# Token weights loaded behind the last quad's keys and queries, zero matmuls only on long-free banks, and a re-planned order in a fused attention and mixer kernel

## The chip, the cores and the metric

One core of one Trainium2 chip. The metric is the device time of one execution in microseconds (us), the median of several. A profiled execution also gives a span, which is about 1.7 us shorter than the metric.

## The reference

Sigmoid attention for 8 batches, 12 heads, 448 positions of 64 features, followed by a token-mixing and a channel-mixing MLP with residuals:

```
scores = q @ k.T / sqrt(64) - log(448);  x = sigmoid(scores) @ v        # x: (8, 448, 768)
h  = relu(x.T @ w_tok1) @ w_tok2                                        # over positions, 256 wide
u  = x + h.T
out = u + relu(u @ w_ch1) @ w_ch2                                       # over channels, 1536 wide
```

## The kernel before

The kernel does not write its instructions in the order of its source. It records operations, each with its engine, an estimated duration, what it waits for and the buffers it uses. A planner then plays them through on estimated times, and the instructions are emitted in the order of the planned starts. Each engine then runs its own list in that order. "Quad" below is four heads: three per batch. The matmuls of scores ("S") and values ("V") use 64x64 tiles of the array, nearly all else the whole array.

The parts that matter:

```python
# Plan: landings of loads, with hitches at some points of the load pipe; landings of what SyncE (SP) issues
self.far, self.load_far, self.sp_wait = 5.0, 2.0, 2.0
self.hitch = [(8.6, 1.1), (15.2, 1.0), (21.9, 0.8)]
...
elif e == "SP":                              # stores, and the transposes done by DMA
    free[e] = t + o.us
    o.end = t + self.far + min(5.0, max(0.0, self.pipe - t - 0.5))
...
self.log.sort(key=lambda o: o.start)         # the order in which everything is emitted
for o in self.log:
    o.emit()

# the kernel: the order of the first loads
load_early(0, "q", "k")
load_early(1, "k", "q")
load_early(0, "v")
tok1_ld = load_w_tok1()
tok2_ld = load_w_tok2()                      # VectorE then spreads it: "spread0/1/6"
load_early(2, "k", "q")
load_early(1, "v")
load_early(2, "v")

# choose(): when nothing else is ready in the first 21 us, a zero matmul (a "fill") keeps TensorE busy
if 3.0 < t < FILL and (not cands or min(c[0] for c in cands) > t + 0.12) and up.start is not None:
    if any(x <= t for x, _ in plan.free_slots("bank", up)):
        o = fill["op"] = filler()            # writes a PSUM bank, reads zeros

# token(b): u becomes fp16 on ScalarE and is transposed by a DMA that SyncE issues; channel1(b) needs all of uT
uT_ops[b].append(op(f"uT_{b}_{blk}", "SP", 1.3, turn, [o], [u16, uT[b]], rank=-1))
```

LEAD and SPAN set how far the scores of batches 2 to 7 run ahead of the mixer work, REST and PAUSE how token-mixing matmuls are spaced. All four only permute work.

## Time and profile before

| | |
|---|---|
| median before the change | 375.59 us (375.43 to 375.96, 3 runs) |
| profiled span | 374.0 us |
| TensorE busy | 366.1 us |
| matmuls, zero matmuls among them | 3,199, of these 20 fills and 7 at the very start |
| TensorE's listed waits | 3.6 us, of these 0.5 us after 45 us |

The prediction shows the lines.

### The profile page before, as it was taken

How to read it: one execution, taken by the hardware profiler on the slowest of the kernel's cores; microseconds unless marked ns; L12 is line 12 of the kernel's file. 1: busy time of each engine (PE TensorE's matmuls, PEld its weight loads, DVE VectorE, ACT ScalarE, POOL GpSimd, SP SyncE). 2: the span in 40 equal slices, each digit the busy share in tenths (PEclk: the TensorE clock that was granted, in tenths of full speed). 3: DMA queues.
4: the chain of work that ended last, by engine and by line, in shares of the span. 5: the costliest groups of instructions: out<-in, count | busy, mean ns of one | idle time of the engine just before them, and what ended most of it. 6: DMA issues, size and time to landing. Idle time of an engine off the chain costs nothing.

```text
span 374.0 us, 7992 instructions
## 1 busy us (share of the span) xinstructions
PE 366.1 (98%) x3199; PEld 187.3 (50%) x3199; DVE 175.7 (47%) x414; ACT 207.6 (56%) x269; POOL 116.0 (31%) x261
## 2 busy tenths in 40 slices
PE   8999999999999999999999999999999999999995
PEld 4455345554454554454445555444455555555653
DVE  4366345654433635552354243934462257665221
ACT  5896993386777877876765576575665321100000
POOL 8873236344444434534444342332000000000000
PEclk9999999999999999999999999999999999999999
DMA  6999999799998999999999999977014363400344
GB/s 102 170 181 206 209 209 183 111 175 178 123 153 147 175 180 137 153 147 227 122 142 131 216 157 193 174 115 107 6 25 104 91 149 88 72 0 2 84 102 110
DMA packets 97013, 50.06 MB, mean 134 GB/s; under 512 B 70544, under 2 KB 93456, under 8 KB 96976
## 3 DMA queue, kind: packets, MB, share of 16 engines
q0 software_dynamic: 24080, 21.62, 42.4%
q1 hardware_dynamic: 72656, 27.62, 41.1%
q8 instruction: 25, 0.41, 0.5%
q10 hardware_dynamic: 240, 0.31, 0.2%
q14 instruction: 12, 0.10, 0.1%
HBM read 43.45 MB, written 11.01 MB: 146 GB/s over the span
## 4 chain that ended last, share of the span: by engine, by line
PE 91%; DMA 3%; POOL 2%; DVE 1%; ACT 1%; issue 1%; SPq 0%; DVEq 0%; POOLq 0%
PE c L1007 30%; PE c L1066 29%; PE qk L578 10%; PE xa L616 8%; PE yn L933 5%; PE k L857 3%; DMA w_tok_s<-in_moe_w_tok_dram 2%; DMA out_dram<-ut 1%; PE xb L675 1%; POOL k L329 1%; PE k L707 1%; PE k L817 1%; PE tk L524 1%; PE k L841 1%; PE yt L891 1%
## 5 line engine op out<-in xcount | busy, mean ns | idle before, releaser
L594 ACT ACTIVATE attn<-qk,att_bias 128x896 f16<-128x896 f32 (+1 forms) x172 | 161.9, 988 | 75.5 <-PE qk L578 75.1
L1007 PE MATMUL c<-uT,w_ch 128*128 128x448 f16 x576 | 119.2, 353 | 0.5 <-DMA out_dram<-ut 0.5
L1066 PE MATMUL c<-w_ch,h2aT 128*128 128x384 f16 x576 | 99.6, 326 | 0.1
L1023 DVE TENSOR_SCALAR h2aT<-c 128x384 f16<-128x384 f32 x96 | 53.5, 557 | 72.9 <-PE c L1007 72.7
L1007 PEld LDWEIGHTS <-w_ch 128*128 128x128 f16 x576 | 52.8, 98 | 57.0 <-issue 12.4
L1066 PEld LDWEIGHTS <-h2aT 128*128 128x128 f16 x576 | 55.0, 98 | 40.8 <-issue 5.9
L1079 DVE TENSOR_TENSOR u<-u,c 128x384 f32<-128x384 f32 x48 | 26.6, 554 | 71.1 <-PE c L1066 65.8
L578 PE MATMUL qk<-qT,kT 64*64 64x448 f16 x672 | 53.5, 363 | 0.6 <-ACT qT L547 0.3
L616 PE MATMUL xa<-attn,v 64*64 64x448 f16 x672 | 36.7, 350 | 0.0
L781 POOL COPY mark<-attn 1x1 f16<-1x1 f16 x54 | 9.6, 178 | 82.8 <-ACT attn L594 80.8
L578 PEld LDWEIGHTS <-kT 64*64 64x64 f16 x672 | 14.9, 104 | 32.7 <-issue 30.1
L496 POOL COPY qp<-q 128x384 f16<-128x384 f16 (+1 forms) x54 | 21.3, 431 | 20.6 <-DMA q<-in_q_dram 13.3
L955 DVE TENSOR_TENSOR u<-x,yn 128x384 f32<-128x384 f16 x48 | 24.7, 548 | 4.8 <-PE yn L933 4.7
L963 ACT ACTIVATE u<-u 128x768 f16<-128x768 f32 x21 | 17.7, 842 | 15.4 <-DVE u L955 15.4
L653 ACT ACTIVATE xT<-xa 128x448 f16<-128x448 f32 (+2 forms) x61 | 22.2, 441 | 6.7 <-PE xa L616 5.4
L616 PEld LDWEIGHTS <-v 64*64 64x64 f16 x672 | 19.5, 107 | 11.9 <-DMA q<-in_q_dram 0.4
L496 POOL COPY kp<-k 128x384 f16<-128x384 f16 (+1 forms) x54 | 21.2, 428 | 10.8 <-DMA k<-in_k_dram 10.8
L933 PE MATMUL yn<-h,w_tok 128*128 128x384 f16 x104 | 21.6, 327 | 0.1
L1023 DVE TENSOR_SCALAR h2odd<-c 128x64 f16<-128x64 f32 x96 | 20.6, 215 | 0.0
L1066 PE MATMUL c<-w_ch,h2odd 128*128 128x384 f16 x96 | 17.1, 326 | 0.1
L340 POOL DMA_DIRECT2D q<-in_q_dram x21 | 15.1, 718 | 6.4 <-issue 6.1
L340 POOL DMA_DIRECT2D k<-in_k_dram x21 | 15.1, 719 | 6.0 <-issue 3.9
(73 smaller groups left out, 207.1 us busy)
## 6 DMA issues: line engine op xcount, KB each, us to landing
out_dram<-u SPq DMA_DIRECT2D x48, 192.0 KB, 3.1
k<-in_k_dram POOLq DMA_DIRECT2D x21, 224.0 KB, 5.1
q<-in_q_dram POOLq DMA_DIRECT2D x21, 224.0 KB, 5.4
v<-in_v_dram POOLq DMA_DIRECT2D x21, 224.0 KB, 5.3
w_ch<-in_moe_w_ch_dram POOLq DMA_DIRECT2D x6, 768.0 KB, 19.2
out_dram<-ut SPq DMA_DIRECT2D x6, 192.0 KB, 4.3
v<-in_v_dram POOLq DMA_DIRECT2D x6, 112.0 KB, 5.6
x<-xT SPq DMA_TRANSPOSE x32, 4.2
```

Of the source, the lines that this page charges most:

```text
L340: nc.gpsimd.dma_start(out=t.ap().rearrange("r h j e -> r h (j e)"), in_=heads.rearrange("(h s) (p j) e -> (s p) h (j e)", s=2, j=J),)
L496: nc.gpsimd.tensor_copy(out=pm[:, to, :, :], in_=src[:, fr, :, :])
L578: nc.tensor.matmul(out=ps[64 * s : 64 * s + 64, h, 0:S], lhsT=kT[64 * h : 64 * h + 64, i, s, :], rhs=qT[64 * h : 64 * h + 64, :, s, :], st ...
L594: nc.scalar.activation(out=at[:, hs, :], in_=ps[:, hs, 0:S], func=SIGMOID, bias=bias_t[:, :], scale=att_scale,)
L616: nc.tensor.matmul(out=ps[s](slice(64 * h, 64 * h + 64)), lhsT=vf[64 * s : 64 * s + 64, h, order[i], :], rhs=attn[i][64 * s : 64 * s + 64, ...
L653: nc.scalar.activation(out=xt[:, s, to : to + n], in_=ps[s](every)[:, fr : fr + n], func=COPYF)
L933: nc.tensor.matmul(out=ps[:, :], lhsT=w_tok2[:, t, s0 : s0 + 2, :], rhs=h1[b][:, t, c], start=(t == 0), stop=(t == 1),)
L955: nc.vector.tensor_tensor(out=to, in0=x, in1=y, op=ADD)
L1007: nc.tensor.matmul(out=ps[:, :], lhsT=w_ch1[cb // 4][:, db, 128 * (cb % 4) : 128 * (cb % 4) + 128], rhs=uT[b][:, db, :], start=(db == 0), ...
L1023: nc.vector.tensor_scalar(out=to, in0=ps[:, fr], scalar1=0.0, scalar2=None, op0=MAX)
L1066: nc.tensor.matmul(out=ps[:, :], lhsT=h, rhs=w, start=(cb == 0), stop=(cb == NCB - 1))
L1079: nc.vector.tensor_tensor(out=t, in0=t, in1=ps[:, :], op=ADD)
```

## The change

It is meant to let the planner fill the early gaps of TensorE with the transposes of the last quad instead of zeros, to keep zero matmuls from standing in front of real work while they wait for a bank, and to plan with landings nearer to the real ones.

```diff
-        self.hitch = [(8.6, 1.1), (15.2, 1.0), (21.9, 0.8)]
+        self.hitch = [(8.6, 1.1), (15.2, 1.4), (19.5, 0.8), (21.9, 0.5)]
...
-    LEAD, SPAN, REST, LATE = 18.0, 0.93, 1.0, 0
-    FILL, UP = 21.0, 7
+    LEAD, SPAN, REST, LATE = 20.0, 0.86, 0.8, 0
+    FILL, UP, SURE = 21.0, 7, 0.8
...
-    PAUSE = 1.0
+    PAUSE = 1.5
...
     load_early(0, "v")
+    load_early(2, "k", "q")
     tok1_ld = load_w_tok1()
     tok2_ld = load_w_tok2()
-    load_early(2, "k", "q")
     load_early(1, "v")
...
-            if any(x <= t for x, _ in plan.free_slots("bank", up)):
+            if any(x <= t - SURE for x, _ in plan.free_slots("bank", up)):
```

## The prediction

> **What bounds the kernel now.** I read the page's first lines, then the chain of waits, then the waits of TensorE, and last the timeline of the first 25 us of all engines. The time is 375.59 us, the profiled span 374.0.
>
> ```profile
> PE 366.1 (98%) x3199; PEld 187.3 (50%) x3199; DVE 175.7 (47%) x414; ACT 207.6 (56%) x269; POOL 116.0 (31%) x261
> PE 91%; DMA 3%; POOL 2%; DVE 1%; ACT 1%; issue 1%; SPq 0%; DVEq 0%; POOLq 0%
> ...
> 342.65 27.31 PE c L1066 x168
> ```
>
> The reader is to see that TensorE (PE) bounds nearly everything: it is busy in 366.1 of 374.0 us and makes 91% of the chain. The last line says how dense it is there: 27.31 us over 168 matmuls of 384 columns is 162.6 ns each. So no wait hides inside the stretches of plain matmuls; only the number of PE instructions, the switches between kinds of work, and PE's few waits can move. Those waits are listed in one view, for the whole run:
>
> ```profile
> PE idle L463 <- DVE att_bias L276: 1.2, 1, 1.2
> PE fill L478 <- DVE xT L647: 0.8, 1, 0.8
> PE c L1007 <- DMA out_dram<-ut: 0.5, 1, 0.5
> PE tk L524 <- issue: 0.3, 1, 0.3
> PE qk L578 <- ACT qT L547: 0.3, 1, 0.3
> PE qk L578 <- ACT uT L761: 0.3, 1, 0.3
> PE k L707 <- DVE h L724: 0.2, 1, 0.2
> ```
>
> They sum to 3.6 us, 1.2 of it the start that the change does not touch. The largest other one, 0.8 us, is what the change aims at. The timeline shows its cause (start, length, engine, line):
>
> ```profile
> 15.57 0.39 PE L478 MATMUL fill<-uT 128*128 128x256 f16 x2
> ...
> 16.21 0.72 PE L478 MATMUL fill<-uT 128*128 128x256 f16 x4
> 16.31 0.83 DVE L382 COPY w_tok<-w_tok_s 128x384 f16<-128x384 f16 x2 [3.21 <-DMA w_tok_s<-in_moe_w_tok_dram]
> ...
> 17.05 1.15 DVE L647 CAST xT<-xa 128x448 f16<-128x448 f32 x2
> ...
> 17.72 0.27 PE L478 MATMUL fill<-uT 128*128 128x256 f16 x1 [0.80 <-DVE xT L647]
> ```
>
> VectorE (DVE) sat 3.21 us for the second token weight to land at 16.3, with the two xT copies behind it in its order, although their matmuls were done by about 15.6. The zero matmul ("fill") wanted a PSUM bank that those copies free, so it stood in front of the next score matmuls until 17.72. ScalarE then lost 1.02 us too: its next sigmoid began at 18.36, after 17.34. Up to 17.34 its sigmoids run without a gap from 6.85, so there ScalarE is the bound and PE's fills cost nothing.
>
> **What the Trainium skill says.** (1) "TensorE: Matmul & The Clock Gate", the part on the array's detail and the step-by-step part: ScalarE and VectorE take their queue strictly in order, and matmuls keep program order, only weight loads being pulled ahead. The trace agrees: the copies waited behind a weight 3.21 us late, the scores behind a fill 0.80 us late. (2) The same page gives N columns / 2.4 GHz + about 2.5 ns for each warm matmul: 162.5 ns for 384 columns; the trace has 162.6. (3) The same page says that an idle window of about 3.4 us can halve the clock, which is why fills exist; this trace grants full clock in every slice and PE's longest wait is 1.2 us, so fewer fills should not cool it. (4) "TensorEngine Tiling (Array Packing)", key properties: changing the tiling mode drains the array. In the trace, from one group of three 448-column matmuls to the next with four 64x64 score matmuls between (chain at 38.53, 39.20, 39.51) takes 0.98 us; 3 x 0.189 + 0.19 (the score group where no switch borders it, at 21.32) is 0.76, so two switches cost 0.22, some 0.11 each.
>
> **The change part by part.** Comparing the built orders (no time in them):
>
> - Removed: fills fall from 20 to 9. All other kinds of PE work have the same counts (3,199 matmuls to 3,188). Four fills between scores at 14.23 to 14.88 took 0.65 us, less one switch of 0.11, so about 0.135 each. 11 x 0.135 = 1.5 us of PE work (1.2 by columns alone). Nine of the eleven stood after 13 us.
> - Switches between 64x64 and full-array work: 217 before, 215 after: 2 x 0.11 = 0.2 us. More groups of scores run straight into their value matmuls (22 against 18), which other splits nearly use up again.
> - Moved: keys and queries of the last quad of batch 0 go ahead of the token weights. Their transposes, 28 matmuls (at 18.79, 19.45 and 20.27: 0.34 + 0.51 + 0.29 = 1.14 us), now stand around the first scores of quad 1, where PE had fills. This is how the fills become useful; it is the same gain as theirs, not another.
> - Waits: VectorE's token-weight spread now stands after the xT copies and the x copy, so the 0.8 us should go. In its place the token weights come later: four loads of 112 KB are put ahead, 448 KB, at the 170 to 180 GB/s of those slices 2.6 us. The second weight then lands at about 16.3 + 2.6 = 18.9 (estimate). By hand along the new order: value matmuls done 15.6, xT copies until 16.9, x transposed 17.5, qT copy to 17.5, x copy to 18.35 (0.76 us); the first token matmul, now only one fill and one score group later, is there at about 17.7 and waits some 0.7. The spread ends at about 19.7, ReLU (0.42), second spread (0.6), second ReLU until 21.2; the first token-2 matmul arrives near 20.7 and waits some 0.5. So 0.8 goes, and 0.5 to 1.2 comes.
> - The planner's other numbers (LEAD, SPAN, REST, PAUSE) only permute PE work from 65 us on. Attention gets somewhat earlier: the scores of batch 6, quad 2 by 9 us of PE work, of batch 7 by 2 to 7. In the old run that quad's last transposed load was issued at 227.23, about 5 us to landing, used near 248: 16 us of slack, 9 of them spent. Some 0 to 0.3 us of new waits.
>
> Sum: -1.5 (fills) -0.2 (switches) -0.8 (the wait) +0.9 (new waits near 18 and 21 us) +0.2 (later) = -1.4 us. 375.59 - 1.4 = 374.2. After 45 us PE waits 0.5 us in all, so what is won at the start should keep to the end; the tail from the last matmul to the last store is unchanged.
>
> **The rivals.**
>
> - *The token weights' lateness eats it all.* For: the load is on the chain now (DMA 6.24 us at 10.05), and it is pushed back 2.6 us. Against: in the old order the first token matmul ran only at 21.8, and there was slack. If the wait is 2 us instead of 1.2, the time is about 375.
> - *Gain larger than the fills.* If the landing is as quick as planned and no new wait stands at 18 us, PE gains 1.5 + 0.2 + 0.8 = 2.5 us, giving 373.1. For: ScalarE also stops losing 1.02 us at 18.36, and bounds PE there.
> - *ScalarE or DMA becomes the bound in the squeezed middle.* ScalarE is busy 66.55 of 100 us between 150 and 250; DMA is at or above 9 tenths in most slices up to 260 us, which speaks for it. But loads are let go by sigmoids three units back, and the slack above is several us. Would add 0.5 to 2 us: 375 to 376.
> - *A colder clock after fewer fills*: would add a us or more at the start; no gap nears the window.
>
> **Range and chances.** The mechanisms move the time between -2.5 and about +0.3 us, so the range is 373.1 to 375.7. A change of 2% would be 7.5 us, while all of PE's waits and fills together are under 7 us: faster by 2% is nearly excluded, and slower by 2% would need a wait of a sort that nothing in the profile hints at.
>
> **What would show it.** Right: 9 fills, PE busy about 364.5 to 365, no fill waiting for xT, ScalarE's gap at 18.36 gone, the first group of 448-column channel matmuls (38.46 before) 1 to 2 us earlier, and a similar lead at 303 us and at the end. The token matmul should wait for the x copy for 0.3 to 1 us, and its second weight matmul for the spread or the ReLU. Wrong: a wait over 1.5 us on a token weight's landing or spread, waits on transposed keys or queries after 150 us, a granted clock under full, or a lead at 45 us that is lost later.

## More of the kernel before

A difference under half a us is near the scatter: the kernel before was between 374.8 and 376.2 us in nearly all of its executions, once 377.7.

One more place turned out to matter, a wait of TensorE (PE) at 174 us. In the kernel before, the timeline of SyncE and of PE there shows (start, length, engine, operation; in brackets the idle time before and its releaser):

```profile
167.25 1.26 SPq L501 DMA_TRANSPOSE qT<-qp  x1
168.60 1.22 SPq L991 DMA_TRANSPOSE uT<-u  x1
169.92 1.19 SPq L1044 DMA_DIRECT2D out_dram<-ut  x2
...
173.99 1.29 PE L1007 MATMUL c<-uT,w_ch 128*128 128x448 f16 x6 [0.52 <-DMA out_dram<-ut]
```

The channel matmuls of batch 3 wait 0.52 us, by the profile for an output store. They do not read what that store moves; what they do read is uT, whose last transpose was issued at 168.60.

## The result, and the profile after

375.23 us (375.05 to 375.62, 6 runs) against 375.69 us (375.35 to 376.03, 6 runs) of the kernel before: ratio 0.9989, 95% interval 0.9976 to 1.0002. Ratios here are the mean time of one kernel's runs over the mean of the runs of the kernel before that are listed beside it, so they are not quite the ratio of the medians. The time lies in the predicted range, 1.0 us above the predicted 374.2.

The page of the changed kernel, its line of engines and its chain:

```profile
PE 365.1 (98%) x3188; PEld 186.6 (50%) x3188; DVE 175.8 (47%) x414; ACT 207.8 (56%) x269; POOL 115.4 (31%) x261
PE 94%; DMA 2%; DVE 2%; ACT 1%; issue 0%; ACTq 0%
```

TensorE has 11 matmuls fewer and is busy 1.0 us less (busy time itself scatters: it is 367.1 us in experiment 8 and 366.0 in experiment 10, whose matmuls are those of the kernel before). The span is 0.6 us shorter. So part of the gain turned into waiting; PE's list of waits in the changed kernel says where:

```profile
PE c L1007 <- DMA uT<-u: 1.2, 1, 1.2
PE idle L463 <- DVE att_bias L276: 1.2, 1, 1.2
PE k L707 <- DVE h L724: 0.4, 1, 0.4
...
PE qk L578 <- ACT attn L594: 0.3, 1, 0.3
...
PE k L707 <- DVE x L691: 0.2, 1, 0.2
```

The fill's wait is gone. The two waits of token matmuls, for x (0.2) and for the ReLU (0.4), are those foreseen near 18 and 21 us. New and not foreseen is the first line. The start itself went as intended; the changed kernel's timeline of VectorE and PE:

```profile
16.20 1.16 DVE L647 CAST xT<-xa 128x448 f16<-128x448 f32 x2 [0.62 <-PE xa L616]
16.38 0.90 PE L578 MATMUL qk<-qT,kT 64*64 64x448 f16 x8
17.21 0.62 PE L675 MATMUL xb<-ident,xT 128*128 128x128 f16 x8
17.87 0.76 DVE L691 COPY x<-xb 128x512 f16<-128x512 f16 x2
18.57 1.04 DVE L382 COPY w_tok<-w_tok_s 128x384 f16<-128x384 f16 x2
```

The xT copies start right after their matmuls, ahead of the token weight's spread, which now starts at 18.57 (before: 16.31). Two score groups stand together at 16.38, the second of which had to wait until 17.92 before. The start of the first channel matmul, before and then after:

```profile
38.46 0.74 PE L1007 MATMUL c<-uT,w_ch 128*128 128x448 f16 x3
```

```profile
37.23 0.74 PE L1007 MATMUL c<-uT,w_ch 128*128 128x448 f16 x3
```

The changed kernel is 1.23 us earlier there, and has one group of two token matmuls more behind it (2 x 0.163 = 0.33 us), so its lead is 1.56 us in these two traces. At the end it is 0.6. Here is what took the rest, SyncE and then PE of the changed kernel:

```profile
172.46 1.18 SPq L1050 DMA_DIRECT2D out_dram<-u  x2
173.73 1.54 SPq L991 DMA_TRANSPOSE uT<-u  x1
175.38 1.25 SPq L501 DMA_TRANSPOSE kT<-kp  x1
176.72 1.24 SPq L991 DMA_TRANSPOSE uT<-u  x1
...
182.62 2.44 PE L1007 MATMUL c<-uT,w_ch 128*128 128x448 f16 x12 [1.21 <-DMA uT<-u]
```

It is the place of the 0.52 us wait before: the first channel matmuls of batch 3. ScalarE had finished the fp16 copy for that last transpose at 174.31 (173.47 + 0.84). SyncE was busy issuing others, each 1.2 to 1.5 us, and issued it at 176.72; it took 5.86 us to land. So the lead should have been lost in SyncE's order; the experiments test this. One of the signs that the prediction had named for being wrong, "a lead at 45 us that is lost later", has come.

### The profile page after: what moved, and what is told of

It is laid out like the page before. It is cut to its first block, busy times and chain, and to the rows that moved or that the text cites. A ratio compares the mean times of both kernels' runs of the same rounds, so it can differ in the third digit from the quotient of the medians.

```text
span 373.4 us, 7967 instructions
## 1 busy us (share of the span) xinstructions
PE 365.1 (98%) x3188; PEld 186.6 (50%) x3188; DVE 175.8 (47%) x414; ACT 207.8 (56%) x269; POOL 115.4 (31%) x261
## 4 chain that ended last, share of the span: by engine, by line
PE 94%; DMA 2%; DVE 2%; ACT 1%; issue 0%; ACTq 0%
PE c L1007 30%; PE c L1066 29%; PE qk L578 11%; PE xa L616 8%; PE yn L933 5%; PE k L857 3%; DMA uT<-u 2%; PE tq L524 1%; PE tk L524 1%; PE xb L675 1%; PE idle L463 1%; ACT attn L594 1%; PE k L817 1%; PE k L841 1%; PE k L707 1%; PE yt L891 1%
```

## The experiments

**Theory A**: the start gained 1 to 1.6 us, and a wait for the last uT transpose of batch 3, caused by SyncE's order, gave most of it back. **Rivals**: B, the DMA engines are saturated there and the landing does not follow the issue; L, the later numbers (LEAD and so on) are what matters; F, the predicted step that zero matmuls are work on the path, so that the gain is their number; K, zero matmuls hold TensorE's clock.

Edits that change only the order are made on the planned list, so everything else keeps its place. Eleven runs, the first eight runs on one chip, the last three on another. All were correct. The first call has 11 runs of the kernel before and the third has 11 of its own; experiments 5 to 8, of the second call, are compared with the 11 of the first call and one more.

**1. One swap on SyncE.**

```diff
-        self.log.sort(key=lambda o: o.start)
+        by = {o.name: o for o in self.log}; by["turnk_5_2"].start = by["uT_3_2"].start + 0.001
+        self.log.sort(key=lambda o: o.start)
```

> Changed kernel, one swap in SyncE's order: the transposed load of batch 5's last keys goes behind the last transpose of batch 3's uT instead of ahead of it; nothing else moves. Theory A (the gain of the start was given back in one 1.2 us wait of the channel matmuls for that transpose, because SyncE issues it 1.3 us late behind the keys): the transpose is issued at about 175.4 instead of 176.7, lands about 181.2, the wait falls from 1.2 us to under 0.2, and the time to about 374.1 (1.1 below the changed kernel, 1.5 below the one before). Theory B (the DMA engines are saturated there, so the landing does not follow the issue): the wait stays at 0.8 us or more, and the time within 0.4 us of the changed kernel. Theory C (the keys then come too late): a new wait of scores on transposed keys near 190 to 200 us.

373.77 us (373.63 to 374.48, 5 runs), ratio 0.9955 (0.9933 to 0.9977). SyncE and PE of this run:

```profile
174.16 3.03 SPq L991 DMA_TRANSPOSE uT<-u  x2
177.29 1.46 SPq L501 DMA_TRANSPOSE kT<-kp  x1
...
181.94 2.26 PE L1007 MATMUL c<-uT,w_ch 128*128 128x448 f16 x11 [0.60 <-DMA uT<-u]
```

The transpose was issued at 175.88 (by the chain of waits), 0.84 us earlier than in the changed kernel, and the wait fell from 1.21 to 0.60: the landing follows the issue. That is theory A, in size half of what it expected. No wait for keys appeared. The median fell by more than that wait: by 1.5 us against the result above and by 2.0 against experiment 2, on the same chip. The profiled execution was the slowest of the five (374.48); what the wait was in the others isn't known.

**2. The changed kernel again**, beside it on the same chip; no edit.

> The changed kernel again, beside the others on the same chip. All theories: 375.2 us, 0.3 to 0.6 under the kernel before. Theory A: the 1.2 us wait of the batch 3 channel matmuls on the uT transpose stands in this profile too (0.8 to 1.6 us). Theory D (that wait was a chance of one execution): it is missing or at another place.

375.73 us (374.89 to 377.73, 6 runs) against 375.45 of the kernel before: ratio 1.0013 (0.9985 to 1.0042). Here no gain is left. The wait for uT is there again, longer, at 1.6 us. Two of the six executions, 377.56 and 377.73, had a mean granted clock of 0.995 and 0.994, the other four 0.997 to 1.0; these two raise the mean. So the change is worth between 0 and 0.5 us, and neither comparison is clear of 1.

**3. Kernel before without its 12 zero matmuls after 13 us.**

```diff
-        self.log.sort(key=lambda o: o.start)
+        self.log = [o for o in sorted(self.log, key=lambda o: o.start)
+                    if o.name[:5] != "fill_" or o.start < 13.0]
```

> Kernel before, with its 12 zero matmuls that stand after 13 us taken out and the order of all else kept. The step of the prediction (11 fills x 0.135 us are work on the path): the time falls by 12 x 0.135 = 1.6 us, to 374.0. Theory S (up to 17.3 us ScalarE is the bound and the fills lie beside it; afterwards the transposed x waits for VectorE, which waits for the second token weight, with or without fills): only the score group at 17.9 gets earlier, the transposes of xT stay at 18.2 and the gain is 0.1 to 0.5 us.

376.38 us (375.12 to 378.85, 6 runs), ratio 1.0024 (0.9990 to 1.0057): no gain, where the predicted step asked for 1.6 us. The windows of this run show a second thing. Columns: stretch, length, busy time of PE, PE's weight loads, VectorE, ScalarE and GpSimd, then the granted clock, DMA share, GB/s.

```profile
15.00:20.00 5.00, 3.52 (x54) 1.88 (x45) 2.98 (x8) 3.94 (x5) 3.79 (x6) 0.89 1.15 171
20.00:25.00 5.00, 4.80 (x62) 2.33 (x58) 2.00 (x4) 3.31 (x4) 4.67 (x7) 0.77 1.18 168
```

And the kernel before, the same stretches:

```profile
15.00:20.00 5.00, 4.21 (x65) 2.16 (x61) 3.20 (x8) 3.77 (x5) 3.76 (x6) 1.00 1.20 178
20.00:25.00 5.00, 4.80 (x67) 2.21 (x66) 2.79 (x6) 4.49 (x5) 3.95 (x6) 1.00 1.18 177
```

Without fills PE was busy only 3.52 of 5 us, and its clock was granted at 0.89 and then 0.77. The six executions, in order of their mean clock over the whole run, took 378.85 us (0.990), 377.41 (0.993), 377.33 (0.995), 375.12 (0.997), 375.26 and 375.42 (0.998 both). The three that stayed nearly warm have a mean of 375.27 us, 0.2 below the 375.46 of the kernel before (its execution of 377.66 left out), and not 1.6. The profile says why. Where the fills stood, PE now waits 1.1 us for sigmoids and 0.7 us for the xT copies. The transposes of xT start 1.4 us after VectorE begins to spread the token weight (17.55 after 16.13); in the three profiles that keep all fills it is 1.9 to 2.0 us (18.24 after 16.31 in the kernel before, 17.65 after 15.61 in experiment 8 and after 15.71 in experiment 10). So the 12 fills held the path up by some 0.5 us there, not by 1.6; the clock fell only after that, at about 19 us. Step F falls and theory S holds: in the old order most of these zeros lay beside ScalarE's work or beside the wait for the token weight. Rival K is supported for that order: the clock sank right behind the place of the fills, and three of six executions had a mean clock of 0.995 or less, which none of the kernel before had in the 23 executions that are listed beside the experiments. But fills are not all of it: kernels with more of them left had such executions too: one of six in experiment 8 (all 20 fills), in 6 (18) and in 4 (9), and two of six in 2 (9).

**4. The changed start with the old later numbers.**

```diff
-    LEAD, SPAN, REST, LATE = 20.0, 0.86, 0.8, 0
+    LEAD, SPAN, REST, LATE = 18.0, 0.93, 1.0, 0
-    PAUSE = 1.5
+    PAUSE = 1.0
```

> The changed kernel with the planner's later numbers (LEAD, SPAN, REST, PAUSE) as they were before: new load order, landings and the rule for zero matmuls stay. Theory A: the start's lead of about 1.3 to 1.8 us is there; whether it is kept hangs on what new waits this order has after 45 us: with none (under 0.3 us) the time is 373.9 to 374.3; with one of about 1 us it is 375.2. Rival theory L (the later numbers are what gained and the start gained nothing that lasts): the time is that of before, 375.6, without a new wait after 45 us.

379.11 us (378.36 to 381.87, 6 runs), ratio 1.0108 (1.0077 to 1.0139): slower by over 1%, outside of what either theory expected. Its first channel matmul is at 37.10, so the start's lead is there. Then three waits take it, among PE's waits of this run:

```profile
PE c L1007 <- DVE u L1079: 1.6, 1, 1.6
...
PE yn L933 <- DVE ut L923: 0.9, 1, 0.9
PE c L1007 <- DMA uT<-u: 0.9, 1, 0.9
```

They sum to 3.4 us. About 1 us of the 2.6 us by which its span (376.6) exceeds that of the kernel before is not explained by waits and lead, and stays open. What the run does show: an earlier start is no gain in itself, because the planner then makes another order of everything later, which meets its own waits. It shows too that the later numbers matter together with the new start: without them the changed kernel is slower by 3.4 us (against experiment 2). The plan itself says as much: built again, its last planned start is at 375.2 us, that of the changed kernel at 369.6.

**5. A store moved behind too.**

```diff
...                                              # last = the latest planned store before uT_3_1
+        by["turnk_5_2"].start, last.start = by["uT_3_2"].start + 0.001, by["uT_3_2"].start + 0.002
```

> As e1_kt_later, and also the store of one block of batch 2 behind the last uT transpose of batch 3. In e1_kt_later the wait was still 0.6 us: that transpose was issued at 175.88 and landed 6.0 us later, though its source was ready near 174.3. Theory A (SyncE's order is the cause): issued about 174.4, landed about 180.4, before PE wants it at 181.3: the wait is gone, time about 373.2 (0.6 under e1_kt_later). Theory B (transposes close together queue up in the DMA engines): issue 1.5 us earlier but landing by less than 0.5, wait still 0.3 to 0.6, time as e1_kt_later, 373.8.

373.95 us (373.56 to 374.55, 6 runs), ratio 0.9956 (0.9934 to 0.9978); span 372.1 against 372.7 in the first experiment. SyncE and PE:

```profile
171.13 4.45 SPq L991 DMA_TRANSPOSE uT<-u  x3
175.68 1.27 SPq L501 DMA_TRANSPOSE kT<-kp  x1
177.04 4.94 SPq L1050 DMA_DIRECT2D out_dram<-u  x4
...
181.35 2.44 PE L1007 MATMUL c<-uT,w_ch 128*128 128x448 f16 x12
```

The wait is gone from the profile, as theory A said, and the span fell by 0.6 us, but the median is not below that of the first experiment: that last step is within the scatter. Not only the issue changed. The last transpose of uT was issued at about 174.4, and with it the landing became quicker: at most 4.3 us here, 3.6 in experiment 9 and 2.8 in experiment 11, against 5.9 to 6.1 in the changed kernel, its repeat and experiment 1. So B is wrong, for the landing does follow the issue, and the earlier issue alone would have done: with a landing of 6.1 us it would still have landed at 180.5, before PE comes at 181.35.

**6. The load order alone**, on the kernel before.

```diff
+    load_early(2, "k", "q")
     tok1_ld = load_w_tok1()
     tok2_ld = load_w_tok2()
-    load_early(2, "k", "q")
```

> Kernel before with the new load order alone, planned again with the old landings and the old rule for zero matmuls; 18 fills. Theory of the prediction (transposes of the last quad become useful work in place of fills, gain as many us as fills go): only 2 fills go, 0.3 us, so 375.2. Rival (the gain is that VectorE no longer holds the xT copies behind the late weight, whatever the fills): the 0.8 us wait of a fill for xT is gone or under 0.4 us, and the first channel matmul starts at 37.5 or earlier instead of 38.46; the end then depends on later waits, each to be read from the list of PE's waits.

375.59 us (374.63 to 379.77, 6 runs), ratio 1.0013 (0.9974 to 1.0051). No fill waits for xT any more, as the rival said, but the first channel matmul is at 38.04 (with the one token group more behind it), not at 37.5. Later waits are 0.9 us for a uT transpose and 0.4 us at batch 3. The execution of 379.77 us had a mean clock of 0.989, with 18 fills in place.

**7. The rule for zero matmuls alone**, on the kernel before.

```diff
-    FILL, UP = 21.0, 7
+    FILL, UP, SURE = 21.0, 7, 0.8
-            if any(x <= t for x, _ in plan.free_slots("bank", up)):
+            if any(x <= t - SURE for x, _ in plan.free_slots("bank", up)):
```

> Kernel before with the rule alone that zero matmuls take only banks free for 0.8 us; 10 fills, 2 of them after 15 us. Theory K (from the run without fills: fills hold PE's granted clock in the stretch where ScalarE is the bound): some executions show a clock of 0.990 to 0.997 over the run, slices under full speed near 15 to 25 us, and times of 376 to 378 beside others near 375. Theory of the prediction (fewer fills do not cool the clock and save 0.135 us each): clock 0.998 or more in all executions and 374.3 to 375.

375.71 us (375.04 to 376.31, 6 runs), ratio 1.0001 (0.9979 to 1.0022), clocks 0.997 to 1.0. First channel matmul at 37.77, again with the token group more. Ten fills less, and the median is no lower, against the prediction's step; but the clock did not sink either (1.00 from 15 to 20 us, with PE busy 3.84 us of the 5), so this run does not bear out K. Its profile has waits of 0.6 us for the xT copies and 0.6 us for sigmoids in the places where fills stood.

**8. The later numbers alone**, on the kernel before.

```diff
-    LEAD, SPAN, REST, LATE = 18.0, 0.93, 1.0, 0
+    LEAD, SPAN, REST, LATE = 20.0, 0.86, 0.8, 0
-    PAUSE = 1.0
+    PAUSE = 1.5
```

> Kernel before with the planner's four later numbers alone (LEAD 20, SPAN 0.86, REST 0.8, PAUSE 1.5). The start is the same instruction by instruction up to about 65 us. Theory A (these numbers gain nothing of themselves, they only pick an order, good or bad by the waits it meets): 375 to 378, and its distance from the kernel before is within 0.6 us of the difference of the two sums of PE's waits after 65 us. Rival L (they are the gain): 375.2 or less without less waiting.

375.83 us (374.88 to 379.96, 6 runs), ratio 1.0024 (0.9983 to 1.0066): nothing gained by these numbers alone, so rival L falls; with the new start they do matter (experiment 4). One execution had a clock of 0.990 and took 379.96, with all 20 fills in place. The trace held a surprise about the start, which is the same, instruction by instruction, as in the kernel before. VectorE and PE of this run:

```profile
15.61 0.83 DVE L382 COPY w_tok<-w_tok_s 128x384 f16<-128x384 f16 x2 [2.06 <-DMA w_tok_s<-in_moe_w_tok_dram]
...
16.58 0.83 PE L478 MATMUL fill<-uT 128*128 128x256 f16 x5
17.34 0.38 PE L578 MATMUL qk<-qT,kT 64*64 64x448 f16 x4
```

The second token weight landed at 15.6 instead of 16.3, and no wait of the fill is listed. The 0.8 us wait on which the prediction built is not in every execution.

**9. Experiment 5 without its two zero matmuls after 13 us**: the log filter of experiment 3 added to the edit of experiment 5.

> As e5_out_later, with the two zero matmuls after 13 us taken out too, order of all else kept. Theory W (in the new order the transposes of the last quad keep PE busy, so the fills are no longer needed for the clock): clock 0.997 or more in all executions and the time within 0.3 us of e5_out_later, 373.9. Theory K (it is the fills that hold the clock): slices under full clock near 15 to 25 us as in e3_before_nofill, and executions of 375 to 377.

373.73 us (373.61 to 373.79, 5 runs), ratio 0.9951 (0.9939 to 0.9963): the fastest kernel, and steady. Clocks 0.997 to 0.999. In the new order PE is busy 4.11 of the 5 us from 15 to 20 (3.52 in experiment 3), and its clock in that stretch and the next is 1.00. That fits theory W, that the moved transposes do there what zeros did. It isn't the whole story of the clock: experiment 2 has the same start, and two of its executions had a low one.

**10. The same kind of swap on the kernel before.**

```diff
...                                              # by and the sort as in experiment 1
+        by["turnq_5_1"].start = by["uT_3_3"].start + 0.001
```

> Kernel before, with one swap on SyncE: the transposed load of batch 5's second queries goes behind the last uT transpose of batch 3. Theory A (the 0.5 us wait at 174 in the kernel before, which the profile names after an output store, is the same dependency as the 1.2 us wait of the changed kernel): the transpose is issued about 1.3 us earlier, the wait is gone, time 0.3 to 0.5 us under the kernel before. Rival (the wait is really for the output store): the wait stays at 0.4 to 0.6 us and the time too.

374.79 us (374.42 to 376.25, 6 runs) against 375.57, ratio 0.9987 (0.9971 to 1.0004). SyncE and PE:

```profile
166.82 1.21 SPq L991 DMA_TRANSPOSE uT<-u  x1
168.12 1.26 SPq L501 DMA_TRANSPOSE qT<-qp  x1
169.47 1.19 SPq L1044 DMA_DIRECT2D out_dram<-ut  x2
...
172.69 1.30 PE L1007 MATMUL c<-uT,w_ch 128*128 128x448 f16 x6
```

The store is still behind the transpose, and the wait has gone. The transpose was issued 1.8 us earlier and landed in 2.7 us, against 5.3 in the kernel before. So the 0.52 us "for the store" was a wait for the uT transpose, the same dependency as the later 1.2 us. The fill waits 0.2 us for xT in this run, a third value for the 0.8. The interval still touches 1, so the gain in time is likely rather than shown.

**11. Experiment 5 again**, beside 9 and 10.

> e5_out_later again on this chip, beside the others: 373.6 to 374.2, 1.3 to 1.8 under the kernel before, no wait for a uT transpose in the profile.

374.02 us (373.77 to 374.18, 5 runs), ratio 0.9958 (0.9944 to 0.9972), no wait for a transpose of uT. With that wait out of both kernels (10 and 11, same chip) the change is worth 374.79 - 374.02 = 0.8 us of medians (1.1 us of means). On the side of the changed kernel a store was moved too, so the two edits are not quite alike.

## Why the prediction was right or wrong

The time was in the range; faster by 2% and slower by 2% were rightly put aside. The centre was 1.0 us too low: a gain of 1.4 us was forecast; 0.46 us was measured, and none in the repeat. The upper end doesn't follow from its own sum either: 375.59 + 0.3 is 375.9, not 375.7. That the sum for the start (1.6 us) came near the measured lead (1.2 us) is partly luck, since its terms were wrong one by one. Step by step:

- *PE is the bound, and only its counts, switches and waits can move.* Right, with one addition: the granted clock can move as well (experiment 3).
- *Fills, -1.5 us (11 x 0.135).* The count was right, the value wrong (and ten of the eleven, not nine, were planned after 13 us: 12 before, 2 after). The prediction contradicts itself here: its first part says that up to 17.34 us ScalarE is the bound "and PE's fills cost nothing", and its sum then prices all eleven as work on the path. Taking 12 fills out of the old order freed some 0.5 us in the trace, and 0.2 us in the time of the executions that stayed warm. In the new order the two late fills did stand on the path: 374.02 to 373.73 without them, 0.15 us each, near the 0.135 of the working (a small difference, but the two runs' executions hardly overlap). What the fills' place is worth depends on what else PE could do there. That the start gains because real transposes, 1.14 us of them, move in is argued, not shown: with the token group counted, the first channel matmul is 0.4 us earlier than in the kernel before with the load order alone (experiment 6), 0.6 with the rule for zeros alone (experiment 7), and 1.2 with all of the change. I had called these two the same gain, and took its size from the wrong one.
- *Switches, -0.2 us.* 215 against 217 by the prediction's count; never separated from the rest. A recount over the built programs, matmuls of 64x64 tiles against all others, gives 222 against 218, so that even the sign of this small term is open.
- *The fill's wait for xT, -0.8 us.* The mechanism is right and the changed kernel has no such wait. The size was one execution: 0.8, none and 0.2 us in three profiles of the same start. First channel matmul at 38.46, 37.87 and 37.87 in these three; at 37.23, 37.05, 37.16, 37.10, 37.24 and 37.50 in the changed kernel and experiments 2, 1, 4, 5 and 11, which start alike. Means 38.07 and 37.21 differ by 0.9 us, with the token group 1.2 us. The two traces compared first had shown 1.56. (The copies were not "3.21 us late" either: that is how long VectorE sat idle; their matmuls were done by about 15.6 and they started at 17.05.)
- *New waits near 18 and 21 us, +0.9.* Measured 0.2 + 0.4 = 0.6. The landing was estimated at 18.9; the spread started at 18.57.
- *Later waits, +0.2 us.* This is the step that failed most. The prediction checked slack for transposed keys and queries, at 227 to 248 us, and never for uT, although PE's list already had a wait at exactly that work, under a store's name. It was 0.52 us and became 1.21 and 1.61 in two profiles of the changed kernel: 0.7 to 1.1 us more. A wait of 0.3 us for a sigmoid at 105 us came on top. Lead of 1.2 less some 1.0 to 1.4 leaves roughly nothing to 0.2 us; measured were 0.46 us and, in the repeat, nothing.
- *Rival "token weights eat it all"*: wrong, there was slack. *Rival "gain larger"*: only with SyncE's order mended, 373.7 to 374.0. *Rival "DMA bounds the squeezed middle"*: it did foresee a loss of this size, but not its kind: what was lost hung on the order of SyncE's issues, and came back when that order alone was changed. The four later numbers, to which I gave the squeeze, gain nothing by themselves (experiment 8), but without them the new start loses (experiment 4). *Rival "colder clock"*: it did not come in the profiled changed kernel. Two executions of its repeat had a low mean clock, and in which stretch is not known.
- *Gap length as the test of the clock.* "No gap nears the window" was the reason to dismiss that rival. Experiment 3 lost clock near 20 us, with no wait of PE over 0.7 us between 5 and 45 us.

Open: why experiment 4 is about 1 us longer than its waits say; which executions lose some clock and where. Why the last uT transpose also landed sooner when less was issued just ahead of it was not tested. The new planned landings (the hitches) were never run alone.

## What to carry to other kernels

Where a planner orders everything, a gain at the start only lasts if the new order meets no new wait; look through the list of waits for small ones that are already at the edge, and ask of each which operand it really waits for. Filler work must be priced by what takes its place, not by its own duration; in one order here the clock sank where it was taken out. A wait seen in one trace needs a second trace before it goes into a sum.

## What the Trainium skill lacked or had wrong

- "TensorE: Matmul & The Clock Gate", the table of idle and busy states in its first part, ties the slow clock to an idle window of about 3.4 us. In experiment 3 the mean clock was 0.89 and 0.77 in two stretches of 5 us while no wait of PE there was longer than 0.7 us and PE was busy 70% of the first stretch (3.52 of 5 us). The page does warn, in its section on a second failure mode, of idle moments between groups of matmuls that are short and frequent. What it lacks is how much short idling is too much; here 3.52 us busy of 5 went with a lower clock and 3.84 (experiment 7) did not, and the runs do not give the threshold.
- "DMA: Bandwidth & Descriptors": I found no time that SyncE needs to issue a transpose within SBUF of a few hundred KB. In the changed kernel it was 1.2 to 1.7 us each in the stretch from 167 to 178 us, and waiting for other issues held the last uT transpose back by 2.4 us. From issue to landing that transpose took 5.9 us there, and 2.8 to 6.1 us over the traces of the same place in the other orders of the changed kernel.
